# Fourier mixing and an ELU layer on one core: products of later x chunks put behind the even/odd products

## The chip, the cores and the metric

The kernel runs on one core of a Trainium2 chip. The time is the device time of one execution in microseconds; before the change the median of three runs is 2578.33 us (2577.13 to 2579.94). Everything is fp32. The engines are called PE (TensorE), DVE (VectorE), ACT (ScalarE), POOL (GpSimd) and SP (SyncE, which here only issues DMAs).

## The reference

```python
def _attn_ref(x, filt_r, filt_i):              # x (8, 3008, 256), filters (1505, 256)
    X = np.fft.rfft(x, axis=1)
    F = (filt_r + 1j * filt_i)[None, :, :]
    y = np.fft.irfft(X * F, n=x.shape[1], axis=1)
    return y.astype(np.float32)

def _moe_ref(x, w_in, w_out):                  # x (24064, 256), w_in (256, 2048), w_out (2048, 256)
    h = x @ w_in
    g = np.where(h > 0.0, h, np.exp(np.minimum(h, 0.0)) - 1.0)
    return (g @ w_out).astype(np.float32)

def reference(...):
    y = _attn_ref(x, filt_r, filt_i)
    return _moe_ref(y.reshape(8 * 3008, 256), w_in, w_out)
```

Each of 8 batches is filtered along its 3008 rows in the frequency domain; the result goes, row by row, through two matrix products with an ELU between them.

## The kernel before

**Mixing.** 3008 is 47 x 64, and the transform is done in two steps by matrix products, forward and back. Per batch there are these stages, and each stage hands over through DRAM:

- `x_load` and `x_unit` (L226, L227): a chunk c of x (6 per batch, four rows of 47 and their mirror images) is loaded, and DVE makes its sum `sd` and difference in place (`xc`), two operations.
- `a_unit` (L233): the first products, `psa <- sd,ta` and `psa <- xc,ta`, in 64x64 tiles, four of them concurrent; ACT copies `psa` to `t1` (L244). It takes two chunks at a time, so four PSUM banks. `z_write` (L322) stores them.
- `z_read` (L328) reads them transposed into `t2`; `b_unit` (L419) makes the second products, `pf <- t,pairs`, in 24x32 tiles with four banks; ACT and DVE take sums out of `pf` (L425 to L430).
- `f_read` (L348, issued by POOL) brings the filter into `fall`. `re_mult`, `re_join`, `re_sums`, `im_mult`, `im_join`, `im_sums` (L433 to L468) multiply with it on DVE. For the first group of a batch, ACT makes one extra copy (L437) in `re_mult`.
- `bi_unit` (L485) makes the first products of the way back, `pv <- zs,pairs`; ACT copies them (L488), `y_write` (L496) stores them.
- `tn_read` and `y_read` (L501, L506) bring them back transposed, `n_unit` (L520) makes the even and odd products `pse` and `pso`, 64x64 tiles again, and ACT copies them to `y` (L526); `n_sums` (L546 to L571) forms their sums on DVE.

The second and third stage go over groups g = 0, 2, 4, 6 of a batch; the last one over six parts m.

**The two layers.** An item is a part m of a batch and a quarter q of the 2048 columns: 192 items. Both products are done with seven block products in place of eight. `up_steps` (L592) gives the seven up steps, into banks `phs` (the "s" bank, four steps that add to it in turn, with an ACT copy, L603, between them), `pha` and `phd`; ELU is made by ACT (L609, L610) and DVE (L600, L614). `down_steps` (L675) gives the seven down steps into `po`. One step is four PE instructions of 256 columns.

**Order.** Everything is written out by hand, each engine works in program order, and so does each DMA queue. The main loop has one quad per item: quad i holds the up steps of item i and the down steps of item i - 1, in an order given by letters, U for up and D for down. 24 quads make a period, in which one batch passes through the layers while the next ones are mixed. `at(quad, place, fn, ...)` puts a unit of the mixing into a quad: place 2 after the third step, 4 a step or two later, 0 in the middle, 3 after the third step of the second half, 1 at the end. In `opens` are the quads that begin with a down step: those behind a unit that took four banks, so that ACT can free them. All of `phs`, `pha`, `phd`, `psa`, `pf`, `pv`, `pse` and `pso` share four banks, which go round. Below, quads are counted within their period of 24.

```python
        for i in range(-PER, len(items) + 3):
            ...
            for n, k in enumerate("DUUDUDDU" if i in opens else "UUDUDDU"):
                ...
                if n == 2 or n == (4 if i in opens else 3):
                    for fn, a in plan.get((i, 2 if n == 2 else 4), ()):
                        fn(*a)
            for fn, a in plan.get((i, 0), ()):
                fn(*a)
            for n, k in enumerate("DUUDUD" if i in opens else "DUUDUDD"):
```

In a period, quads 0, 3 and 4 end with `a_unit` of two chunks of the batch that is mixed (2, 3, 4 for batch 1, the first one done this way), with both `x_unit`s in the middle of the same quads. Quads 6, 10, 14 and 18 end with `b_unit`, quads 9, 13, 17 and 21 with `bi_unit`, then `y_write` and, at quad 21, `y_read` of part 0. `n_unit` of part 0 stands at place 2 of quad 23, parts 1 and 2 at the end of quads 1 and 5, parts 3, 4 and 5 in the middle of quads 8, 12 and 16.

Of the kernel before, what the change touches and what calls it, by code (L numbers as in the profile page):

```python
# [28 lines left out]
B = 8  # L29
# [4 lines left out]
NXC = H // XC  # L34
NG = K2 // 4
XBUFS = 4
# [101 lines left out]
def kernel(  # L138
# [9 lines left out]
    nc = tc.nc  # L148
# [83 lines left out]

    def a_unit(b, c):  # L233
        ps = [[bank("psa") for _ in range(2)] for _ in range(2)]
        for j in range(2):
            xt, w, sm = xs.pop((b, c + j)), tas.pop((b, c + j)), sds.pop((b, c + j))
            for u in range(2):
                for o, src in ((0, sm), (64, xt[:, 1])):
                    for (_, p), r in zip(ps[j], HALVES):
                        nc.tensor.matmul(p[o:o + 64, u, :], w[r, u, o:o + 64], src[r, u, :], start=True, stop=True)  # L240
        for j in range(2):
# [82 lines left out]
    def z_read(b, g):  # L324
        t = t2[:, g % 2]
        for p in range(4):
            k = p * K2 + 4 * g
            nc.sync.dma_start(t[32 * p:32 * p + 24].rearrange("i u d -> i (u d)"),  # L328
                              zs[b][:, k:k + 4, :].rearrange("i u d -> i (u d)"))

# [14 lines left out]
    def f_read(b, g):  # L345
        t = fbufs[g % 2]
        for a in range(4):
            nc.gpsimd.dma_start(t[32 * a:32 * a + 24].rearrange("p c u d -> p (c u d)"),  # L348
                                fp[g, a].rearrange("q c u d -> q (c u d)"))

# [161 lines left out]
    def n_unit(b, m):  # L512
        t, w, h = t4s.pop((b, m)), tns.pop((b, m)), half(m)
        ps = [bank(n) for n in ("pse", "pso")]
        for q, i in enumerate(order(m)):
            n = 32 if i == 0 else 64
            for dh in range(2):
                for o in (0, 64):
                    for (_, p), r in zip(ps, HALVES):
                        nc.tensor.matmul(p[o:o + 64, dh, ds(64 * q, n)], t[r, i - 4 * m, ds(dh * P + o, 64)],  # L520
                                         w[r, i - 4 * m, 0:n], start=True, stop=True)
# [196 lines left out]
    def o_unit(b, m):  # L718
# [9 lines left out]
        o = o.rearrange("p (u f k) e s -> p u f k (e s)", u=4, f=2)  # L728
        queues = itertools.cycle((nc.sync, nc.scalar) if (b, m) == (B - 1, 5) else (nc.sync,))
        for k in range(2):  # L730
# [100 lines left out]
    with tc.manual_schedule():  # L831
# [160 lines left out]
        for i in range(2):  # L992
            at(4, 0, nc.gpsimd.memset, fbufs[i], 0.0)
        STEP = ((1, 2), (1, 1), (1, 1), (2, 2), (2, 2), (2, 1), (3, 2))
        STEP_LAST = ((1, 2), (1, 1), (2, 3), (2, 2), (2, 2), (2, 1), (3, 2))
        for b in range(B):
            t = (b - 1) * PER
            if b > 0:
                for c, s in enumerate((2, 2, 3, 3, 4, 4) if b == 1 else (0, 0, 3, 3, 4, 4)):
                    if b > 1:  # L1000
                        at(t + s, 0, x_unit, b, c)
                    elif c % 2 == 0:
                        for k in (c, c + 1):
                            at(s - 1, 1 if c else 2, x_unit, b, k)
                    if c % 2 == 0:
                        opens.add(t + s + 1)
                        at(t + s, 1, a_unit, b, c)
                    nb, nxt = (b, c + XBUFS) if c + XBUFS < NXC else (b + 1, c + XBUFS - NXC)
                    if nb < B:
                        at(t + s, 1, x_load, nb, nxt)  # L1010
                    at(t + s, 1, z_write, b, c)
                for g in range(0, NG, 2):
                    s = t + 6 + 2 * g
                    opens.update((s + 1, s + 4))
                    for k in (g, g + 1):
                        at(s - 2, 1, f_read, b, k)
                        at(s - 1, 0, z_read, b, k)
                    at(s, 1, b_unit, b, g)
                    for fn, (d, place), a in zip((re_mult, re_join, re_sums, im_mult, im_mult, im_join, im_sums),
# [4 lines left out]
            for m, (s, place, sums) in enumerate(((23, 2, ((23, 0, 0, 1), (23, 3, 2))), (25, 1, ((25, 1),)), (29, 1, ((29, 1),)),  # L1024
# [3 lines left out]
                if (b, m) == (0, 1):  # L1028
                    pass
                elif b > 0 or m > 0:  # L1030
                    r = 21 if m == 0 else s - 2
                    at(t + r, 0, tn_read, b, m)
                    at(t + r, 1 if m == 0 else 0, y_read, b, m)
                    at(t + s, place, n_unit, b, m)

                    for q, p, *a in sums:
                        at(t + q, p, n_sums, b, m, *a)
# [74 lines left out]
```

## Time and profile before

| what | us |
|---|---|
| median of the runs | 2578.33 |
| the profiled execution, its own time | 2575.46 |
| its span | 2573.7 |
| one period of 24 quads | 310.0 |
| large products: one instruction of 128x128 by 256 columns, mean duration | 0.377 |
| waits of PE for another engine or a DMA after the first 300 us, sum | 1.5 |
| longest of PE's waits, all at the start: phd for DVE (12 times) | 11.4 in all, 5.0 the longest |
| groups of psa: 672 instructions, 21 groups | 82.0 (sum of the busy time of both kinds) |
| groups of pse and pso: 3008 instructions, 47 groups | 108.3 (the same) |
| groups of pf, pv: 952 instructions each, 28 groups each | 39.0, 33.0 |

Busy times of single kinds overlap where tiles run side by side, and matmuls are pipelined, so a duration is longer than the distance between two starts; distances are read from the timeline. The groups of one line are found by their tile names. A wait is put down to the engine or the DMA that ended it.

### The profile page before, as it was taken

How to read it: one execution, taken by the hardware profiler on the slowest of the kernel's cores; microseconds unless marked ns; L12 is line 12 of the kernel's file. 1: busy time of each engine (PE TensorE's matmuls, PEld its weight loads, DVE VectorE, ACT ScalarE, POOL GpSimd, SP SyncE). 2: the span in 40 equal slices, each digit the busy share in tenths (PEclk: the TensorE clock that was granted, in tenths of full speed). 3: DMA queues.
4: the chain of work that ended last, by engine and by line, in shares of the span. 5: the costliest groups of instructions: out<-in, count | busy, mean ns of one | idle time of the engine just before them, and what ended most of it. 6: DMA issues, size and time to landing. Idle time of an engine off the chain costs nothing.

```text
span 2573.7 us, 44194 instructions
## 1 busy us (share of the span) xinstructions
PE 2529.4 (98%) x16732; PEld 2160.7 (84%) x16732; DVE 2071.6 (80%) x3612; ACT 1528.2 (59%) x2698; POOL 189.3 (7%) x325
## 2 busy tenths in 40 slices
PE   8889999999999999999999999999999999999998
PEld 5678889888898888988889888888888888898887
DVE  4988887788877888788887888778887788876666
ACT  4665665666556555665556656565656665555554
POOL 3421100010000000000000000000010011000000
PEclk8999999999999999999999999999999999999999
DMA  8753213522234231433215231243213322110010
GB/s 209 207 146 76 68 23 84 138 69 56 48 87 123 56 74 44 113 83 74 61 40 143 71 81 36 72 124 82 56 48 80 85 62 68 36 46 19 19 28 17
DMA packets 229288, 196.38 MB, mean 76 GB/s; under 512 B 129050, under 2 KB 202748, under 8 KB 228980
## 3 DMA queue, kind: packets, MB, share of 16 engines
q1 hardware_dynamic: 215828, 167.62, 26.7%
q0 software_dynamic: 12096, 25.68, 3.5%
q8 instruction: 132, 2.16, 0.3%
q14 instruction: 80, 0.66, 0.1%
q10 hardware_dynamic: 1152, 0.26, 0.1%
HBM read 121.60 MB, written 74.97 MB: 76 GB/s over the span
## 4 chain that ended last, share of the span: by engine, by line
PE 88%; DVE 6%; ACT 2%; DMA 2%; issue 1%; SPq 0%; POOL 0%; DVEq 0%; POOLq 0%; ACTq 0%
PE po L675 41%; PE phs L592 23%; PE phd L592 12%; PE pha L592 6%; PE pse L520 2%; PE pf L419 1%; PE psa L240 1%; PE pv L485 1%; DVE g L600 1%; DVE g L614 1%; DMA ff<-in_filt_i_dram 1%; ACT e L610 1%; ACT e L609 1%; PE pso L520 0%; DMA x<-in_x_dram 0%
## 5 line engine op out<-in xcount | busy, mean ns | idle before, releaser
L675 PE MATMUL po<-g,wo 128*128 128x256 f32 (+1 forms) x5376 | 1316.8, 377 | 0.0
L675 PEld LDWEIGHTS po<-g,wo 128*128 128x128 f32 x5376 | 1013.5, 190 | 165.2 <-issue 49.4
L603 ACT ACTIVATE g<-phs 128x512 f32<-128x512 f32 (+1 forms) x576 | 338.6, 588 | 717.2 <-PE phs L592 716.1
L592 PE MATMUL phs<-y,wi 128*128 128x256 f32 (+1 forms) x2288 | 580.7, 376 | 1.5 <-DVE g L614 1.1
L610 ACT ACTIVATE e<-e 128x512 f32<-128x512 f32 (+1 forms) x768 | 477.1, 621 | 24.3
L592 PEld LDWEIGHTS phs<-y,wi 128*128 128x128 f32 x2288 | 430.5, 190 | 56.5 <-ACT g L603 1.8
L600 DVE TENSOR_TENSOR g<-phd,g 128x512 f32<-128x512 f32 (+1 forms) x384 | 258.9, 674 | 267.0 <-ACT e L610 196.8
L609 ACT ACTIVATE e<-g 128x512 f32<-128x512 f32 (+1 forms) x576 | 353.4, 614 | 66.3 <-DVE g L600 51.2
L614 DVE SCALAR_TENSOR_TENSOR g<-e,g 128x512 f32<-128x512 f32 (+1 forms) x576 | 387.8, 673 | 1.6 <-ACT e L610 0.9
L614 DVE SCALAR_TENSOR_TENSOR g<-e,phs 128x512 f32<-128x512 f32 (+1 forms) x192 | 129.7, 675 | 139.2 <-ACT e L610 139.2
L592 PE MATMUL phd<-y,wi 128*128 128x256 f32 (+1 forms) x768 | 196.3, 378 | 11.4 <-DVE g L600 11.4
L592 PE MATMUL phs<-ys,wi 128*128 128x256 f32 (+1 forms) x784 | 198.7, 376 | 6.4 <-ACT g L603 5.6
L592 PE MATMUL phd<-ys,wi 128*128 128x256 f32 (+1 forms) x768 | 193.8, 375 | 0.0
L592 PE MATMUL pha<-ys,wi 128*128 128x256 f32 (+1 forms) x752 | 190.0, 375 | 0.0
L609 ACT ACTIVATE e<-phs 128x512 f32<-128x512 f32 (+1 forms) x192 | 113.3, 590 | 113.2 <-PE phs L592 113.2
L592 PEld LDWEIGHTS phd<-y,wi 128*128 128x128 f32 x768 | 145.7, 191 | 32.2 <-DVE g L600 16.1
L592 PEld LDWEIGHTS phs<-ys,wi 128*128 128x128 f32 x784 | 147.6, 190 | 25.2 <-ACT g L603 7.8
L348 POOL DMA_DIRECT2D fall<-fp x224 | 110.0, 499 | 692.0 <-DVE r L458 686.4
L592 PEld LDWEIGHTS phd<-ys,wi 128*128 128x128 f32 x768 | 145.7, 190 | 16.6
L592 PEld LDWEIGHTS pha<-ys,wi 128*128 128x128 f32 x752 | 142.8, 190 | 16.5
L600 DVE TENSOR_TENSOR g<-pha,g 128x512 f32<-128x512 f32 (+1 forms) x192 | 129.0, 672 | 24.3 <-PE pha L592 24.3
L654 DVE TENSOR_TENSOR g<-g,g 128x512 f32<-128x512 f32 (+1 forms) x192 | 132.6, 690 | 6.6
(184 smaller groups left out, 2175.4 us busy)
## 6 DMA issues: line engine op xcount, KB each, us to landing
t<-yd SPq DMA_DIRECT2D x94, 256.0 KB
z<-t SPq DMA_DIRECT2D x84, 256.0 KB
fall<-fp POOLq DMA_DIRECT2D x224, 96.0 KB, 2.9
t<-z SPq DMA_DIRECT2D x224, 96.0 KB
yd<-t SPq DMA_DIRECT2D x112, 192.0 KB
out_dram<-o SPq DMA_DIRECT2D x632, 32.0 KB
xc<-in_x_dram SPq DMA_DIRECT2D x84, 128.0 KB
xc<-in_x_dram SPq DMA_DIRECT2D x161, 64.0 KB
```

The lines of the kernel that those rows point to most:

```text
L240: nc.tensor.matmul(p[o:o + 64, u, :], w[r, u, o:o + 64], src[r, u, :], start=True, stop=True)
L348: nc.gpsimd.dma_start(t[32 * a:32 * a + 24].rearrange("p c u d -> p (c u d)"), fp[g, a].rearrange("q c u d -> q (c u d)"))
L419: nc.tensor.matmul(pf[p][1][32 * a:32 * a + 32, js, :], fb[r, v, :], t2[r, js, a, :], start=True, stop=True, tile_position=(32 * p, 32 * a))
L520: nc.tensor.matmul(p[o:o + 64, dh, ds(64 * q, n)], t[r, i - 4 * m, ds(dh * P + o, 64)], w[r, i - 4 * m, 0:n], start=True, stop=True)
L592: nc.tensor.matmul(ps[:, a, 0:h], w_in[q][:, COMBO[n], a, :], y[n], start=start and a == 0, stop=True, skip_group_check=True)
L600: nc.vector.tensor_tensor(out=g[o], in0=i0, in1=i1, op=ALU.add)
L603: nc.scalar.activation(out=g[o], in_=i0, func=AXT.Copy)
L609: nc.scalar.activation(out=e, in_=src, func=AXT.Relu, scale=-1.0)
L610: nc.scalar.activation(out=e, in_=e, func=AXT.Exp, scale=-1.0)
L614: nc.vector.scalar_tensor_tensor(out=g[n], in0=es[n], scalar=1.0, in1=src, op0=ALU.subtract, op1=ALU.max)
L654: nc.vector.tensor_tensor(out=g["t4"], in0=g["b21"], in1=g["t2"], op=ALU.subtract)
L675: nc.tensor.matmul(po[i][:, u, 0:h], w_out[q][:, COMBO[n], a, :], g[n][:, a, :], start=begin and a == 0 and n in (1, 3, 6, 4), stop=True, ...
```

## The change

Batch 1 stays as it is. From batch 2 on (`AFTER = 2`) a chunk of x is multiplied singly, right behind an `n_unit` of an earlier batch: chunks 0 to 3 behind parts 2 to 5 of the batch two before, chunks 4 and 5 behind parts 0 and 1 of the batch before. The quads are `AQ`, and all of these stand at place 1: 5, 8, 12, 16, 22 and 1 of a period. `n_unit`s with no chunk behind them (from part 2 of batch 6 on) stay where they were. `x_unit` goes to the quads of `AU`, one chunk each. The quads behind these groups begin with a down step. `b_unit` of groups 2, 4 and 6 moves from the end of its quad to a new place 5, behind the first down step of the next one, whose order becomes DDUUDUDU; what is planned for place 2 of such a quad is then issued after the first up step. The second half of `im_mult` moves from place 2 to place 3 for groups 0, 2 and 4. `z_read` and `f_read` bring both halves of a pair in one DMA per quarter. `n_unit` issues the odd product's tile ahead of the even one's each time. The last part's stores go over three queues.

```diff
-    def a_unit(b, c):
-        ps = [[bank("psa") for _ in range(2)] for _ in range(2)]
-        for j in range(2):
+    def a_unit(b, c, n):
+        ps = [[bank("psa") for _ in range(2)] for _ in range(n)]
+        for j in range(n):
...
     def z_read(b, g):
-        t = t2[:, g % 2]
         for p in range(4):
             k = p * K2 + 4 * g
-            nc.sync.dma_start(t[32 * p:32 * p + 24].rearrange("i u d -> i (u d)"),
-                              zs[b][:, k:k + 4, :].rearrange("i u d -> i (u d)"))
+            nc.sync.dma_start(t2[32 * p:32 * p + 24].rearrange("i g u d -> i (g u d)"),
+                              zs[b][:, k:k + 8, :].rearrange("i u d -> i (u d)"))
...
     def f_read(b, g):
-        t = fbufs[g % 2]
         for a in range(4):
-            nc.gpsimd.dma_start(t[32 * a:32 * a + 24].rearrange("p c u d -> p (c u d)"),
-                                fp[g, a].rearrange("q c u d -> q (c u d)"))
+            nc.gpsimd.dma_start(fall[32 * a:32 * a + 24, 0:2].rearrange("p g c u d -> p g (c u d)"),
+                                fp[g:g + 2, a].rearrange("g q c u d -> q g (c u d)"))
...
-                    for (_, p), r in zip(ps, HALVES):
+                    for (_, p), r in reversed(tuple(zip(ps, HALVES))):
                         nc.tensor.matmul(p[o:o + 64, dh, ds(64 * q, n)], t[r, i - 4 * m, ds(dh * P + o, 64)],
                                          w[r, i - 4 * m, 0:n], start=True, stop=True)
...
-        queues = itertools.cycle((nc.sync, nc.scalar) if (b, m) == (B - 1, 5) else (nc.sync,))
+        queues = itertools.cycle((nc.sync, nc.scalar, nc.gpsimd) if (b, m) == (B - 1, 5) else (nc.sync,))
...
-        STEP = ((1, 2), (1, 1), (1, 1), (2, 2), (2, 2), (2, 1), (3, 2))
+        AFTER = 2
+        AQ, AU = (5, 8, 12, 16, 22, 25), (5, 6, 10, 14, 22, 24)
+        STEP = ((1, 2), (1, 1), (1, 1), (2, 2), (2, 3), (2, 1), (3, 2))
...
-            if b > 0:
+            if 0 < b < AFTER:
                 for c, s in enumerate((2, 2, 3, 3, 4, 4) if b == 1 else (0, 0, 3, 3, 4, 4)):
...
-                        at(t + s, 1, a_unit, b, c)
+                        at(t + s, 1, a_unit, b, c, 2)
+                    if c + XBUFS < NXC:
+                        at(t + s, 1, x_load, b, c + XBUFS)
...
+                    at(t + s, 1, z_write, b, c)
+                if b + 1 == AFTER:
+                    for c, s in enumerate((3, 5, 7, 9)):
+                        at(t + s, 0, x_load, b + 1, c)
+            elif b > 0:
+                for c, s in enumerate(AQ):
+                    s += t - PER
+                    at(AU[c] + t - PER, 0, x_unit, b, c)
+                    opens.add(s + 1)
                     nb, nxt = (b, c + XBUFS) if c + XBUFS < NXC else (b + 1, c + XBUFS - NXC)
                     if nb < B:
-                        at(t + s, 1, x_load, nb, nxt)
-                    at(t + s, 1, z_write, b, c)
+                        at(s, 1, x_load, nb, nxt)
+            if b > 0:
                 for g in range(0, NG, 2):
                     s = t + 6 + 2 * g
                     opens.update((s + 1, s + 4))
-                    for k in (g, g + 1):
-                        at(s - 2, 1, f_read, b, k)
-                        at(s - 1, 0, z_read, b, k)
-                    at(s, 1, b_unit, b, g)
+                    at(s - 2, 1, f_read, b, g)
+                    at(s - 1, 0, z_read, b, g)
+                    at(*((s + 1, 5) if g else (s, 1)), b_unit, b, g)
...
+                    nb, c = b + (2 if m > 1 else 1), m - 2 if m > 1 else 4 + m
+                    if AFTER <= nb < B:
+                        s = AQ[c] + (nb - 2) * PER - t
+                        place = 1
                     at(t + s, place, n_unit, b, m)
+                    if place == 1 and AFTER <= nb < B:
+                        at(t + s, 1, a_unit, nb, c, 1)
+                        at(t + s, 1, z_write, nb, c)
...
-            for n, k in enumerate("DUUDUDDU" if i in opens else "UUDUDDU"):
+            late = plan.get((i, 5), ())
+            for n, k in enumerate("DDUUDUDU" if late else "DUUDUDDU" if i in opens else "UUDUDDU"):
                 s = ups if k == "U" else downs
                 if s:
                     s.pop(0)()
+                if n == 0:
+                    for fn, a in late:
+                        fn(*a)
```

More of the change, by code (lines that the diff above doesn't have):

```diff
@@ L240, in a_unit @@
                         nc.tensor.matmul(p[o:o + 64, u, :], w[r, u, o:o + 64], src[r, u, :], start=True, stop=True)
-        for j in range(2):
+        for j in range(n):
             t = t1s[b, c + j] = t1p.tile([P, XC, D], FP32, tag="t1", name="t1")
@@ L1006 @@
                         opens.add(t + s + 1)
-                        at(t + s, 1, a_unit, b, c)
+                        at(t + s, 1, a_unit, b, c, 2)
+                    if c + XBUFS < NXC:
+                        at(t + s, 1, x_load, b, c + XBUFS)
+                    elif b + 1 < AFTER:
+                        at(t + s, 1, x_load, b + 1, c + XBUFS - NXC)
+                    at(t + s, 1, z_write, b, c)
[7 more added lines that the diff above has]
+                    opens.add(s + 1)
                     nb, nxt = (b, c + XBUFS) if c + XBUFS < NXC else (b + 1, c + XBUFS - NXC)
                     if nb < B:
-                        at(t + s, 1, x_load, nb, nxt)
-                    at(t + s, 1, z_write, b, c)
+                        at(s, 1, x_load, nb, nxt)
+            if b > 0:
                 for g in range(0, NG, 2):
```

## The prediction

> **What bounds the kernel now.** I read the page first: sections 1, 2 and 4.
>
> ```profile
> PE 2529.4 (98%) x16732; PEld 2160.7 (84%) x16732; DVE 2071.6 (80%) x3612; ACT 1528.2 (59%) x2698; POOL 189.3 (7%) x325
> ...
> PEclk8999999999999999999999999999999999999999
> ...
> PE 88%; DVE 6%; ACT 2%; DMA 2%; issue 1%; SPq 0%; POOL 0%; DVEq 0%; POOLq 0%; ACTq 0%
> ```
>
> TensorE is never free, its clock is granted in full, and it holds 88% of the chain of waits. Only work taken off PE, or a new wait put on it, can move the time. Busy time by stretch, over two whole periods of 24 quads:
>
> ```profile
> 408.80:718.77 309.97, 309.75 (x2098) 265.87 (x2097) 255.46 (x447) 186.43 (x330) 18.03 (x36) 1.00 0.31 77
> 1338.70:1648.72 310.02, 309.80 (x2097) 265.94 (x2096) 255.45 (x447) 186.44 (x330) 18.04 (x36) 1.00 0.31 77
> ```
>
> Columns: us, then busy PE, weight loads, DVE, ACT, POOL, then clock. A period is 310 us with 0.22 us of PE idle. The waits of PE after 300 us sum to 1.5 us; nearly all others lie before 230 us. So the steady state has nothing to win but PE's own overheads. These show in PE's timeline, around an x product (psa) and an even/odd product:
>
> ```profile
> 1038.35 1.89 PE L675 MATMUL po<-g,wo 128*128 128x256 f32 x8
> 1040.17 0.43 PE L240 MATMUL psa<-sd,ta 64*64 64x256 f32 x2
> ...
> 1040.43 0.38 PE L240 MATMUL psa<-sd,ta 64*64 64x256 f32 x2
> ...
> 1040.65 0.38 PE L240 MATMUL psa<-sd,ta 64*64 64x256 f32 x2
> ...
> 1042.05 1.02 PE L675 MATMUL po<-g,wo 128*128 128x224 f32 x4
> 1042.91 0.92 PE L592 MATMUL phs<-y,wi 128*128 128x224 f32 x4
> ```
>
> A 256-column instruction takes a 0.216 us slot (four starts per 0.863 us), so the eight of L675 end at 1040.08. The next large product starts at 1042.05, and its four take 0.86 us where 0.756 is normal for 224 columns. The group thus costs 1.97 + 0.10 = 2.08 us. Its work is 8 sets of four concurrent tiles at 0.216 = 1.73. The other 0.35 us is entry and exit: 0.09 before, about 0.05 in the first set, 0.09 after the last, 0.10 in the next product.
>
> **The change, part by part.**
>
> (1) *Chunks behind the even/odd products.* Batches 2 to 7 have 18 pair groups now; afterwards 36 single chunks stand inside even/odd groups that exist anyway. Work unchanged, 18 x 0.35 = 6.3 us of entries removed. Each of 36 seams costs between 0 (sets follow each other at their pace) and a whole entry, 0.35. Both neighbours are 64x64 tiles, so I take the near end, 0.03: 1.1 us. Net -5.2 (bounds -6.3 and +6.3).
>
> (2) *The product of m = 0 moves from three steps into quad 23 to the end of quad 22.* Its rows come by y_read, queued on SP behind y_write:
>
> ```profile
> 1315.46 3.02 SPq L496 DMA_DIRECT2D yd<-t  x4
> 1321.92 1.09 SPq L506 DMA_DIRECT2D t<-yd  x2
> 1323.13 8.63 SPq L735 DMA_DIRECT2D out_dram<-o  x16
> ```
>
> y_write waits for ACT's copies of pv, y_read for y_write to land. The second y_read's semaphore is complete at 1326.61 in the trace's records. Quad 23 begins at 1325.35; the product ran at 1328.03, so it had 1.4 us in hand. Moved, it is due at 1325.44. Quads 21 and 22 keep length and chain (pv starts 13.26 us before quad 23, in every batch), so PE waits. Completion after the start of quad 23, batches 1 to 6: 1.23, 1.20, 1.65, 1.26, 2.61, 1.12 us, the large ones where an instruction fetch delayed packets. Less the entry of 0.09: 8.5 us in all. Bounds 0 (landed in time) and 9.5. Behind it on PE stand the chunk and the first down step; DVE and ACT run dry, nobody catches up, and SP's z_write and x_load behind the chunk only start later, with quads to spare.
>
> (3) *Six more quads begin with a down step* (6, 9, 13, 17, 23, 2 of a period, in place of 1, 4, 5), so they end with one down step less. In quad 6 that brings pf, and with it quad 7, 0.86 us closer to the last up step. Quad 7 has no room:
>
> ```profile
> 1432.45 1.06 ACT L437 ACTIVATE r<-fall 32x1024 f32<-32x1024 f32 x1 [1.91 <-DVE r L430]
> 1433.42 0.57 ACT L603 ACTIVATE g<-phs 128x512 f32<-128x512 f32 x1
> ```
>
> That copy of phs ends at 1433.99; the up step that needs its bank starts at 1434.06. L437 waits for DVE's four sums from pf. The first of these started at 1429.63, 0.3 to 0.4 us after DVE had finished the quad before (L654 at 1428.65); it waited for ACT's copies of pf. With pf 0.86 earlier DVE itself is the limit and gains only 0.38, so PE waits 0.48. Five batches (in batch 1 DVE binds there anyway): 2.4 us, bounds 0 and 3. In the other five (pv at the end of 9, 13 and 17, nothing of the mixing at the end of 23 and 2) the banks come free in time as they do in quads 10, 14 and 18 now; 0.
>
> (4) *Middle pf groups after the first down step, order DDUUDUDU.* Same groups, same entries. But one down step, not two, now separates the second "s" step from the third. Copy: 0.20 us until ACT starts, 0.60 long, 0.05 to PE, 0.85 against a step of 0.863. The same case stands in quad 7, where the fourth step has the margin of (3):
>
> ```profile
> 1432.33 1.89 PE L675 MATMUL po<-g,wo 128*128 128x256 f32 x8
> 1434.06 1.11 PE L592 MATMUL phs<-y,wi 128*128 128x256 f32 x4
> 1435.01 1.03 PE L675 MATMUL po<-g,wo 128*128 128x256 f32 x4
> ```
>
> The four in the middle last 1.11 us where others last 1.03; 0.95 us to the next start where 0.863 is the slot, so 0.085 is lost. 3 x 7 quads x 0.085 = 1.8 us, bounds 0 and 2. The re_mult now ahead of the pha sum on DVE delays that sum by 2.4 us; the exponential that needs it has its next cover in ACT's 0.8 us wait for phs, so 0.
>
> (5) *x_unit in quads 5, 6, 10, 14, 22, 0.* Two DVE operations of 0.69, 1.3 us. DVE idles before its phd sum 4.5, 0.7, 2.4, about 2.2, 3.5 and 0.5 us there (quad 0 gives up one of two). Quad 6 gets 1.7 us more time ahead of that sum from the chunk and the down step. 0; without the cover up to 0.6 x 24 = 14 us, the third rival. The half of im_mult moved behind the phs maximum fills ACT's 0.8 us wait and makes up for the even/odd product gone from the middle of quads 8, 12 and 16 (1.29 us of PE against 1.2 of DVE): 0.
>
> (6) *Merged reads.* Eight z reads take SP 3.2 us and eight fall reads POOL 3.9; half the issues remain, each with twice the bytes. They land quads before their use. 0 both ways. *Odd ahead of even* changes only order: 0.
>
> (7) *Start.* DVE binds quads 7 to 9 (PE lost 0.9 + 1.6 + 0.9 us there). Two chunks, 1.73 us of PE, move in under it, while quad 9's down step ahead gives 0.86 back: -0.9, bounds -2 and +2.
>
> (8) *Tail.*
>
> ```profile
> 2567.52 3.68 SPq L735 DMA_DIRECT2D out_dram<-o  x8
> ```
>
> ACT's queue issues eight more in 3.81 us; the span ends 2.4 us after. With three queues SP has six, 2.8 us: -0.9. POOL's five need 5 x 0.5 and 2.9 us to land by the fall reads, 3.5 by the ff reads at start: between -1.0 and 0. I take -0.8. The Trainium skill (DMA: Bandwidth & Descriptors, Specifications) has about 1 us to the first byte on the GpSimd path against 0.6 on the others; by it 0.4 less would be gained. No row here has the two paths side by side.
>
> **Sum.** -5.2 + 8.5 + 2.4 + 1.8 - 0.9 - 0.8 = +5.8 us. The profiled execution took 2575.46 (span 2573.7 and 1.8 around it), so 2581.3 by its measure. It lies 2.9 below the median 2578.33; against the median, 2584.
>
> **Rivals.**
>
> A, *y_read lands in time*: the chain pv, y_write, y_read shortens by 1.3 us, and (2) is gone: 2584 - 8.5 = 2575.6, and 2571 if (3) and (4) vanish too. For it: y_write's 3.0 us of issue and 3 of landing are far more than its 768 KB need. Against: nothing in the change touches them, and seven batches repeat them within 0.1 us but for the two fetches. [...]
>
> B, *the seam is not free*: at 0.2 us a seam (1) removes 18 x 0.35 = 6.3 and adds 36 x 0.2 = 7.2 us, a loss of 0.9 in place of a gain of 5.2: 2590. From 0.175 on, the regrouping loses. Against: both neighbours are 64x64.
>
> C, *DVE late by x_unit*: 0.3 us in half of the 24 places of quads 6, 10, 14 and 0, 3.6 us: 2588. Against: the idle times of (5).
>
> D, *it does not do what it says*: PE keeps an entry of its own for each chunk, 36 x 0.35 = 12.6 against 6.3 removed: 2596. The 64x64 form on both sides speaks against it.
>
> **How the numbers follow.** Forecast 0.46 (own range 2579 to 2588), A 0.36, B 0.09, C 0.06, D 0.03. Where the chains run faster than I read them, (3) and (4), both of borderline size, go with (2) more often than not: 0.20 of A lies at 2571, 0.16 at 2576. The predicted time is the forecast's. The range takes in A's deeper half and B: 2571 to 2591, about one in ten beyond each end. 0.2%, 5.2 us, is about what a measurement of this kernel can tell from no change, so the bounds are 2573.2 and 2583.5. Faster: 0.20. Same: 0.16 of A and 0.14 of the forecast, whose lower part lies below 2583.5. Slower: the forecast's other 0.32 and B, C, D, 0.50.
>
> **What would show it.** Eighteen groups of psa alone gone, psa behind pso at 64x64 pace. PE waiting at L520 for t<-yd once a period, at the end of quad 22. PE waiting for L603 in quad 7 by about half a microsecond. A period near 311.2 us where it was 310. If the waits of PE show no L520 line, (2) is wrong and A holds; if psa starts later than 0.1 us behind pso, B or D.

## The result, and the profile after

The changed kernel takes 2591.57 us (median of six runs, 2587.04 to 2594.2) against 2578.76 us for the kernel before in the same session: a ratio of 1.0048, 95% interval 1.0038 to 1.0058. It is slower by 12.8 us. The forecast had been 2584 us, the range 2571 to 2591: the sign was right, the size was not, and the time lies just past the upper end.

The page of the changed kernel, sections 1, 2 and 4:

```profile
PE 2530.5 (98%) x16732; PEld 2157.2 (83%) x16732; DVE 2074.3 (80%) x3612; ACT 1528.6 (59%) x2698; POOL 147.6 (6%) x218
...
PEclk8899999999999999999999999999999999999999
...
PE 82%; DVE 9%; ACT 4%; DMA 3%; issue 2%; SPq 1%; POOL 0%; DVEq 0%; POOLq 0%; ACTq 0%
```

PE issues the same 16732 instructions and is busy only 1.1 us longer, while the span is 17.1 us longer (2590.8 against 2573.7). So the work did not grow: PE waits more. Its share of the chain of waits went from 88% to 82%, DVE's from 6% to 9%. Two whole periods (columns as before: us, then busy PE, weight loads, DVE, ACT, POOL, then clock):

```profile
731.93:1043.51 311.58, 309.65 (x2097) 265.52 (x2096) 255.71 (x447) 186.35 (x330) 11.65 (x20) 1.00 0.33 77
1355.10:1666.70 311.60, 309.66 (x2098) 265.51 (x2097) 255.69 (x447) 186.35 (x330) 11.65 (x20) 1.00 0.33 77
```

A period is 1.6 us longer than before (310.0), and 1.9 us of it is now without PE work where 0.2 us was. The waits of PE after 300 us (line, what ended the wait, us in all, times, longest):

```profile
PE pso L518 <- issue: 5.1, 4, 1.3
PE pso L518 <- DMA out_dram<-o: 2.7, 2, 1.3
PE phd L590 <- DVE g L598: 2.5, 10, 0.5
PE phs L590 <- ACT g L601: 1.6, 5, 0.3
```

Before, the only such line was 1.5 us for phd. (Lines L590 and L673 are now the up and the down steps, L601 the copy of phs, L598 and L612 DVE's sum and maximum.) The two lines of L518 are one wait, six times 1.2 to 1.3 us, at the product of part 0. The first label names no cause and the second a store of the layers' output, which this product doesn't read; the queue of SP and the timeline of PE show whose wait it is:

```profile
1329.54 3.01 SPq L494 DMA_DIRECT2D yd<-t  x4
1336.04 1.13 SPq L504 DMA_DIRECT2D t<-yd  x2
```

```profile
1338.79 0.81 PE L673 MATMUL po<-g,wo 128*128 128x256 f32 x3
1340.94 0.24 PE L518 MATMUL pso<-tn,t 64*64 64x64 f32 x1 [1.34 <-DMA out_dram<-o]
```

The semaphore of the second y_read, issued at 1336.58, is complete at 1340.80 in the trace's records, 4.2 us after its issue (before the change it was 4.2 us too, from 1322.43 to 1326.61), and the product starts 0.14 us later. The chain y_write, y_read, product runs as it did before, only PE now arrives first.

The total has to be cut into what the change did and what differs from run to run. Up to the end of quad 4 PE, ACT and DVE have the same work in the same order in every kernel of this study (but for the order of the tiles in one even and odd product; some loads are merged or issued at other moments). The start of quad 5, read at its first up step, lay between 160.9 and 167.0 us in their thirteen profiles, 160.9 in the profile of before (the lowest of all) and 166.7 in the profile after. From there to the end of the last product the times are 2404.5 us before and 2415.2 us after, and the rest of the span 8.3 and 8.9 us. The change thus costs 10.7 + 0.6 = 11.3 us by the traces; of the 17.1 us between the two spans 5.8 lie in the start, where kernels with equal code vary as much, and of the 12.8 us between the medians 11.3 can be found in the traces. The other 1.5 stay open.

### The profile page after: what moved, and what is told of

It is laid out like the page before. It is cut to its first block, busy times and chain, and to the rows that moved or that the text cites. A ratio compares the mean times of both kernels' runs of the same rounds, so it can differ in the third digit from the quotient of the medians.

```text
span 2590.8 us, 43720 instructions
## 1 busy us (share of the span) xinstructions
PE 2530.5 (98%) x16732; PEld 2157.2 (83%) x16732; DVE 2074.3 (80%) x3612; ACT 1528.6 (59%) x2698; POOL 147.6 (6%) x218
## 4 chain that ended last, share of the span: by engine, by line
PE 82%; DVE 9%; ACT 4%; DMA 3%; issue 2%; SPq 1%; POOL 0%; DVEq 0%; POOLq 0%; ACTq 0%
PE po L673 38%; PE phs L590 22%; PE phd L590 11%; PE pha L590 5%; DVE g L612 2%; DVE g L598 1%; PE pso L518 1%; PE pv L483 1%; PE psa L240 1%; ACT e L608 1%; ACT e L607 1%; PE pf L417 1%; DVE g L651 1%; DVE g L649 1%; DVE g L648 0%
## 5 line engine op out<-in xcount | busy, mean ns | idle before, releaser
L673 PE MATMUL po<-g,wo 128*128 128x256 f32 (+1 forms) x5376 | 1320.1, 377 | 0.0
L673 PEld LDWEIGHTS po<-g,wo 128*128 128x128 f32 x5376 | 1013.9, 190 | 170.8 <-issue 34.4
L601 ACT ACTIVATE g<-phs 128x512 f32<-128x512 f32 (+1 forms) x576 | 338.9, 588 | 714.1 <-PE phs L590 713.2
L590 PE MATMUL phs<-y,wi 128*128 128x256 f32 (+1 forms) x2288 | 582.3, 377 | 3.2 <-ACT g L601 1.8
L590 PEld LDWEIGHTS phs<-y,wi 128*128 128x128 f32 x2288 | 429.4, 190 | 63.4 <-ACT g L601 9.1
L598 DVE TENSOR_TENSOR g<-phd,g 128x512 f32<-128x512 f32 (+1 forms) x384 | 259.2, 675 | 277.2 <-ACT e L608 166.4
L612 DVE SCALAR_TENSOR_TENSOR g<-e,g 128x512 f32<-128x512 f32 (+1 forms) x576 | 388.0, 674 | 3.1 <-ACT e L608 1.0
L612 DVE SCALAR_TENSOR_TENSOR g<-e,phs 128x512 f32<-128x512 f32 (+1 forms) x192 | 129.6, 675 | 141.8 <-ACT e L608 141.8
L590 PE MATMUL phd<-y,wi 128*128 128x256 f32 (+1 forms) x768 | 196.7, 379 | 11.7 <-DVE g L598 11.7
L590 PE MATMUL phs<-ys,wi 128*128 128x256 f32 (+1 forms) x784 | 199.8, 377 | 7.8 <-ACT g L601 7.4
L590 PE MATMUL phd<-ys,wi 128*128 128x256 f32 (+1 forms) x768 | 193.8, 375 | 0.0
L590 PE MATMUL pha<-ys,wi 128*128 128x256 f32 (+1 forms) x752 | 190.0, 375 | 0.0
L590 PEld LDWEIGHTS phd<-y,wi 128*128 128x128 f32 x768 | 145.7, 191 | 33.3 <-DVE g L598 17.2
L590 PEld LDWEIGHTS phs<-ys,wi 128*128 128x128 f32 x784 | 147.9, 191 | 29.1 <-ACT g L601 12.1
L590 PEld LDWEIGHTS phd<-ys,wi 128*128 128x128 f32 x768 | 145.8, 190 | 16.5
L590 PEld LDWEIGHTS pha<-ys,wi 128*128 128x128 f32 x752 | 142.9, 190 | 16.5
L598 DVE TENSOR_TENSOR g<-pha,g 128x512 f32<-128x512 f32 (+1 forms) x192 | 128.9, 671 | 23.3 <-PE pha L590 23.3
L652 DVE TENSOR_TENSOR g<-g,g 128x512 f32<-128x512 f32 (+1 forms) x192 | 132.6, 691 | 6.7
L649 DVE TENSOR_TENSOR g<-g,g 128x512 f32<-128x512 f32 (+1 forms) x192 | 130.7, 681 | 6.6
```

Source lines behind the costliest of these rows:

```text
L590: nc.tensor.matmul(ps[:, a, 0:h], w_in[q][:, COMBO[n], a, :], y[n], start=start and a == 0, stop=True, skip_group_check=True)
L598: nc.vector.tensor_tensor(out=g[o], in0=i0, in1=i1, op=ALU.add)
L601: nc.scalar.activation(out=g[o], in_=i0, func=AXT.Copy)
L612: nc.vector.scalar_tensor_tensor(out=g[n], in0=es[n], scalar=1.0, in1=src, op0=ALU.subtract, op1=ALU.max)
L649: nc.vector.tensor_tensor(out=b12, in0=b22, in1=b12, op=ALU.subtract)
L652: nc.vector.tensor_tensor(out=g["t4"], in0=g["b21"], in1=g["t2"], op=ALU.subtract)
```

## The experiments

The theory: the regrouping itself saves time (all 18 groups of psa alone are gone), and it is the waits made by it, each at its own place, that outweigh it. The rivals: the regrouping itself costs (the seams), or it is another part of the change, the merged reads, the late pf or the moved half of im_mult. Where a time "from quad 5 on" is given, it ends with the last product. Before: 2404.5 us.

**e1, all parts but the regrouping.**

```diff
-        AFTER = 2
+        AFTER = 8
-                if b + 1 == AFTER:
+                if b + 1 == AFTER < B:
```

> The changed kernel with all its parts but the regrouping: the chunks of batches 2 to 7 stand in pairs again, in groups of their own, and the even and odd products back in their old places. Theory, by the sums from the two traces: a period of 310.0 to 310.3 us (0.09 us of waits in each of three late quads, 0.13 saved in each late pf group), the small stalls of batch 7's period (0.4 to 0.6 us in quads 9, 13, 17) there as in the changed kernel, so 2579 to 2583. Rival, that the merged reads, the late pf or the moved half of im_mult cost the time: 2588 to 2592, near the changed kernel. Boot: the first up step starts near 79.7 us if the 3.8 us more of the changed kernel's profile are chance, near 83.5 if something in the change does it.

Measured: 2593.54 us, ratio 1.0059 (1.0044 to 1.0074); from quad 5 on 2418.5 us; a period of 312.1 us. The theory is wrong and the rival holds in kind, with a time 1.5 us above the one it gave: without the regrouping the kernel is as slow as with it. The waits of PE after 300 us:

```profile
PE phd L590 <- DVE g L598: 7.9, 26, 0.5
```

In each period PE waits for phd in quads 9, 13 and 17. From start to start, less the steps' own slots, that costs 0.63, 0.43 and 0.44 us (idle, as the profile counts it, 0.47, 0.27 and 0.27), each with 0.1 behind it and 0.1 in the third up step. These are the waits that the changed kernel has in batch 7's period alone, where no chunks are left to be regrouped. The rival names three parts, one of which the prediction had costed at nothing; e5 settles which it is. The start (up to the first up step, equal code) gave 80.6 us here and 83.6 in e3.

**e2, two queues for y.** Both the last group's stores and part 0's loads:

```diff
-            nc.sync.dma_start(y_rows(b, p, 4 * g, 8), t[32 * p:32 * p + 24])
+            queue = nc.gpsimd if g == 6 and p % 2 else nc.sync
+            queue.dma_start(y_rows(b, p, 4 * g, 8), t[32 * p:32 * p + 24])
...
+            queue = nc.gpsimd if m == 0 and k else nc.sync
+            queue.dma_start(t[r], yds[b][k:P:2, 4 * m:4 * m + 4, :])
```

> The changed kernel, but the four stores of y of a batch's last group and the two loads of part 0 behind them are shared out between SP's queue and POOL's, half and half. Theory: PE waits at the odd product of part 0 (1.1 to 1.3 us, six times) because y_write's 3.0 us of issue and y_read's 1.1 stand in one queue; halved, the rows land 1.5 to 2 us earlier, the waits go, 7 us less: 2584 to 2586. Rival 1: the latency decides and not the issue, POOL's path is the longer one: the wait stays or grows, 2591 or more. Rival 2: the wait goes and the next one takes its place (DVE's sums for the first up step of the next item, or the copies of quad 23): 2588 to 2591.

Measured: 2588.64 us, ratio 1.0037 (1.0023 to 1.0052). The waits fell to about half. The waits of PE after 300 us (here L520 is the odd product), SP's queue and POOL:

```profile
PE pso L520 <- issue: 4.1, 6, 0.8
```

```profile
1323.63 0.74 SPq L495 DMA_DIRECT2D yd<-t  x2
1329.15 0.50 SPq L506 DMA_DIRECT2D t<-yd  x1
```

```profile
1323.91 1.26 POOL L495 DMA_DIRECT2D yd<-t  x2 [66.60 <-ACT t L486]
1329.64 0.56 POOL L506 DMA_DIRECT2D t<-yd  x1 [4.48 <-DMA yd<-t]
```

The stores are all issued 1.5 us after the first one began (1323.63 to 1325.17) in place of 3.0. But from there to the first load's issue it is now 4.0 us (1329.15) where it was 3.5, and from that issue to the product 5.1 us (1334.21) where it was 4.9. About half of the issue time saved came back as a longer landing, so the cause of (2) is right, and it is no matter of issue alone. The Trainium skill (DMA: Bandwidth & Descriptors, Specifications) gives the GpSimd path the longer time to the first byte; the direction agrees, though these rows cannot part it from the load on the DMA engines.

**e3, another order for quads 6 and 23.** They open with a down step as in the changed kernel, and end with two as before the change:

```diff
-            for n, k in enumerate("DDUUDUDU" if late else "DUUDUDDU" if i in opens else "UUDUDDU"):
+            early_d = i in opens and i > 5 and i % PER in (6, 23)
+            for n, k in enumerate("DDUUDUDU" if late else "DUUDUDU" if early_d else "DUUDUDDU" if i in opens else "UUDUDDU"):
...
-            for n, k in enumerate("DUUDUD" if i in opens else "DUUDUDD"):
+            for n, k in enumerate("DUUDUD" if i in opens and not early_d else "DUUDUDD"):
```

> The changed kernel with quads 6 and 23 of each period in the order DUUDUDU DUUDUDD: they begin with a down step as in the changed kernel and end with two, as before the change. Theory: the wait of quad 7 for the copy of phs falls from 0.47 to 0.09 us, that of quad 0 from 0.23 to 0, and each of the two quads gets a wait of 0.09 itself, since one down step stands where two did between two steps of phs: 0.4 us less per period, 2 to 4 us in all with the start (2588 to 2590). Rival: the wait of quad 7 hangs on DVE's work (the two x_units), not on the down step: it stays at 0.47 and the time rises by 1 us.

Measured: 2587.06 us, ratio 1.0032 (1.002 to 1.0043); from quad 5 on 2410.9 us, 4.3 less than the changed kernel. PE in quad 7, the changed kernel first, then e3:

```profile
1444.52 1.89 PE L673 MATMUL po<-g,wo 128*128 128x256 f32 x8
1446.73 1.13 PE L590 MATMUL phs<-y,wi 128*128 128x256 f32 x4 [0.31 <-ACT g L601]
```

```profile
1127.92 1.89 PE L673 MATMUL po<-g,wo 128*128 128x256 f32 x8
1129.65 1.12 PE L590 MATMUL phs<-y,wi 128*128 128x256 f32 x4
```

From start to start it was 2.21 us and is 1.73, which is eight slots of 0.216. The wait hung on the down step, not on DVE's work. The wait of 0.23 us in quad 0 went as well. The period gained 0.6 to 0.7 us where I had expected 0.4: a first product behind such a wait also starts 0.1 us late, which I had left out.

**e4, two small parts undone.**

```diff
-        queues = itertools.cycle((nc.sync, nc.scalar, nc.gpsimd) if (b, m) == (B - 1, 5) else (nc.sync,))
+        queues = itertools.cycle((nc.sync, nc.scalar) if (b, m) == (B - 1, 5) else (nc.sync,))
...
+        STEP7 = ((1, 2), (1, 1), (1, 1), (2, 2), (2, 2), (2, 1), (3, 2))
...
-                                                 STEP_LAST if g == 6 else STEP, ((), (), (), (0,), (1,), (), ())):
+                                                 STEP_LAST if g == 6 else STEP7 if b == B - 1 else STEP, ((), (), (), (0,), (1,), (), ())):
```

> The changed kernel with two of its small parts undone: the last stores on two queues, and for batch 7 alone the half of im_mult at place 2 again. Theory: from the end of the last product to the end of the span 8.3 us in place of 8.9, and the waits of PE in quads 9, 13 and 17 of batch 7's period (0.62, 0.43, 0.43) gone: 2 us less, 2589.5. Rival for the tail: the third queue has nothing to do with it and the last leg stays at 8.9 or more. Rival for the waits: they come from the opened quads or the late pf and stay.

Measured: 2589.7 us, ratio 1.0042 (1.0027 to 1.0057). No wait for DVE is left in quads 9, 13 and 17 of batch 7; its period went from 306.97 to 304.82 us, and the end of the span from 8.86 to 8.28 us behind the last product. Both parts as the theory had it, 2.7 us in the trace.

**e5, chunks in pairs, the half of im_mult back at place 2, two queues at the end.**

```diff
-        AFTER = 2
+        AFTER = 8
-        STEP = ((1, 2), (1, 1), (1, 1), (2, 2), (2, 3), (2, 1), (3, 2))
+        STEP = ((1, 2), (1, 1), (1, 1), (2, 2), (2, 2), (2, 1), (3, 2))
...
+        queues = itertools.cycle((nc.sync, nc.scalar) if (b, m) == (B - 1, 5) else (nc.sync,))
```

> As e1 (chunks in pairs again), and besides the half of im_mult of groups 0 to 4 back at place 2 and the last stores on two queues: what is left of the change is the late pf, the merged reads and odd ahead of even. Theory: e1's waits for phd in quads 9, 13 and 17 (0.6, 0.4, 0.4 us in each period, with as much as 0.2 more behind each) come from the moved half of im_mult meeting the even and odd products in the middle of those quads; they go, and a period takes 309.9 to 310.1 us, 2577 to 2580 in all, as before the change. Rival, that the late pf or the merged reads make DVE late there: a period of 311 us or more, 2586 or more.

Measured: 2579.19 us, ratio 0.9996 (0.9987 to 1.0006). A period:

```profile
723.98:1033.85 309.87, 309.64 (x2098) 265.05 (x2097) 255.92 (x447) 186.88 (x330) 11.60 (x20) 1.00 0.35 77
```

So the 2 us per period of e1 were that half of im_mult, and the merged reads, the late pf and the order of odd and even cost nothing together: the period is 0.1 us shorter than before the change.

**e6, part 0 back in the middle of quad 23.** Chunk 4 stays alone at the end of quad 22.

```diff
-                    opens.add(s + 1)
+                    if c != 4:
+                        opens.add(s + 1)
...
-                        s = AQ[c] + (nb - 2) * PER - t
-                        place = 1
+                        r = AQ[c] + (nb - 2) * PER
+                        if m > 0:
+                            s, place = r - t, 1
                     at(t + s, place, n_unit, b, m)
-                    if place == 1 and AFTER <= nb < B:
-                        at(t + s, 1, a_unit, nb, c, 1)
+                    if AFTER <= nb < B:
+                        at(r, 1, a_unit, nb, c, 1)
```

> The changed kernel with the product of part 0 back in the middle of quad 23, where it stood before; its chunk, number 4, stays at the end of quad 22 alone, and quad 23 begins with an up step as before. Theory: the six waits for y_read (1.1 to 1.3 us each) go, and the wait of 0.23 us in quad 0 with them; the lone chunk has an entry of 0.35 us of its own: a period 1.2 us shorter, 310.3 us, 2584 in all. Rival 1, y_read is late in the middle of quad 23 too, since the transfers changed: waits for it stay. Rival 2, the regrouping itself costs time: a period stays above 311 us although the waits are gone.

Measured: 2581.31 us, ratio 1.0013 (1.0004 to 1.0023); a period of 310.2 us. The waits of PE after 300 us have no pso line left:

```profile
PE phd L590 <- DVE g L598: 2.6, 10, 0.5
PE phs L590 <- ACT g L601: 1.6, 5, 0.3
```

This one undoing takes 1.4 us from each period; from quad 5 on 7.9 us. The median fell by 10.3 us; what it fell beyond the 7.9 is in no part of the trace that this edit touches.

**e7, e6 with quad 6's order of e3 and both parts of e4.**

```diff
+            early_d = i in opens and i > 5 and i % PER == 6
...
+        STEP7 = ((1, 2), (1, 1), (1, 1), (2, 2), (2, 2), (2, 1), (3, 2))
...
+        queues = itertools.cycle((nc.sync, nc.scalar) if (b, m) == (B - 1, 5) else (nc.sync,))
```

> As e6, and besides quad 6 in the order DUUDUDU DUUDUDD, the half of im_mult of batch 7 at place 2, and the last stores on two queues. Theory: all the new waits found are out, the saving of five shared groups per period is left: a period of 309.8 us, the tail as before, 2578 to 2580 in all, that is about the time before the change (within 0.1%). Rival: what the regrouping saves is still outweighed, 2583 or more, since the start (x_unit of batch 2 in quads 5 and 6, where DVE is the bound) costs more than thought.

Measured: 2577.05 us, ratio 0.999 (0.998 to 0.9999); a period of 309.8 us, from quad 5 on 2402.4. What is left of the change is a gain of 2.1 us from quad 5 on.

**e8, chunk 4 in the group of part 0 again, but behind the first down step of quad 23.** The group moves from the end of quad 22 to place 5 of quad 23, with y on two queues (e2), quad 6 in the order of e3, and both parts of e4:

```diff
-                    opens.add(s + 1)
+                    if c != 4:
+                        opens.add(s + 1)
...
-                        at(s, 1, x_load, nb, nxt)
+                        at(*((s + 1, 2) if c == 4 else (s, 1)), x_load, nb, nxt)
...
                         s = AQ[c] + (nb - 2) * PER - t
                         place = 1
+                        if m == 0:
+                            s, place = s + 1, 5
...
-                        at(t + s, 1, a_unit, nb, c, 1)
+                        at(t + s, place, a_unit, nb, c, 1)
```

> The changed kernel with chunk 4 still in one group with the odd and even products of part 0, but behind the first down step of quad 23 (0.86 us later, order DDUUDUDU), and the stores and loads of y before it on two queues as in e2; quad 6, batch 7's im_mult and the tail as in e7. Theory: e2 left waits of 0.6 to 0.8 us for y_read; 0.86 us of a down step ahead covers them. A period of 309.9 us, 2578 to 2580 in all. Rival: the copies of four banks then stand between the first up steps of quad 23, and the waits come back there, at phs for ACT: a period above 310.5 us.

Measured: 2575.97 us, ratio 0.9989 (0.9979 to 0.9999). A period of 309.93 us; no wait for y above 0.1 us is left, only the 0.23 us in quad 0 (0.33 with what follows).

**e9, e8 with the sums of part 0 earlier on DVE.**

```diff
-                            s, place = s + 1, 5
+                            s, place, sums = s + 1, 5, ((23, 4, 0, 1), (23, 0, 2))
```

> As e8, and the sums of part 0 on DVE one place earlier each (the first four behind the fourth step of quad 23, the last two in its middle in place of behind the phs maximum). Theory: the wait of 0.23 us in quad 0 (0.33 with what follows it) comes from those last two sums, which stand ahead of the phd sum at the end of quad 23 and so put off the exponential and, behind it on ACT, the copy of phs; the DVE idle time of 3.2 us in the middle of quad 23 takes them up. A period of 309.6 us and 2 us less than e8: 2574, 0.2% under the kernel before the change. Rival: the wait comes from the down step that quad 23 lacks at its end and stays: 309.93.

Measured: 2576.3 us, ratio 0.9988 (0.9979 to 0.9997). In the profile the period is what the theory said, though the 2 us less than e8 do not show in the medians:

```profile
726.13:1035.71 309.58, 309.35 (x2098) 265.24 (x2097) 255.94 (x447) 186.41 (x330) 13.49 (x23) 1.00 0.34 77
```

```profile
PE phd L592 <- DVE g L600: 1.6, 7, 0.2
```

Its waits are those of the kernel before again. So the wait in quad 0 needs both the missing down step (e3 put it back, and the wait went) and the order of DVE (e9). DVE at the end of quad 23 in the changed kernel, columns start, duration, line:

```profile
1353.98 0.69 DVE L612 SCALAR_TENSOR_TENSOR g<-e,phs 128x512 f32<-128x512 f32 x1 [0.80 <-ACT e L608]
1354.59 0.38 DVE L568 TENSOR_TENSOR ys<-ys,y 128x224 f32<-128x224 f32 x1
1354.89 0.38 DVE L569 TENSOR_TENSOR ys<-ys,y 128x224 f32<-128x224 f32 x1
1355.19 0.68 DVE L598 TENSOR_TENSOR g<-phd,g 128x512 f32<-128x512 f32 x1
```

The two sums stand for 0.6 us between the maximum and the phd sum; ACT's exponential and, behind it, its copy of phs come 0.6 us later, of which PE loses 0.23. From quad 5 on e9 takes 2400.9 us, 3.6 less than before, the lowest of all kernels here. The medians of e8 and e9 (2575.97 and 2576.3) cannot be told apart; both are faster than the kernel before, by 0.11% and 0.12%, with intervals that only just leave out no change.

**e10, batch 2's first two x_units on POOL.**

```diff
-        eng = nc.gpsimd if b == 1 and c < XSUMS else nc.vector
+        eng = nc.gpsimd if b == 1 and c < XSUMS or b == 2 and c < 2 else nc.vector
```

> As e9, and the x_units of batch 2's first two chunks, which fall into quads 5 and 6 where DVE binds, on POOL (1.4 to 1.7 us an operation there for 0.69 on DVE). Theory: these two take 1.3 us each from DVE in the stage that it binds; quads 5 to 8 become 1.3 to 2.6 us shorter, 2572. Rival 1: POOL's sums come late for the chunk at the end of the quad, or slow DVE down by sharing its port: no gain or a loss of up to 2 us. Rival 2: another wait binds these quads (ACT's copies of pf): no change.

Measured: 2577.34 us, ratio 0.9991 (0.9982 to 1.0). Quads 5 to 9 take 14.47, 13.12, 10.83, 16.18 and 13.51 us where e9 has 14.35, 13.12, 10.82, 16.18 and 13.51. The x_units were no burden there. Both rivals allow for no gain, and nothing here parts them; that ACT's copies bind these quads is not shown. The prediction's rival C (DVE late by x_unit) falls by the waits of the changed kernel itself: after 300 us PE waits for DVE in quad 21, as before the change, and in batch 7's quads 9, 13 and 17, and nowhere in quads 6, 10, 14 and 0. One wait for y of 0.6 us came back in this profile, at part 0 of one batch, so the cover that the down step gives is thin.

**e11, even ahead of odd again.**

```diff
-                    for (_, p), r in reversed(tuple(zip(ps, HALVES))):
+                    for (_, p), r in zip(ps, HALVES):
```

> As e9, with the even product's tile ahead of the odd one's each time, as before the change. Theory: only the order of four tiles that run side by side, no change (a shared group 2.10 us, the lone even and odd product 1.18). Rival: with odd ahead the last tile and the first of the chunk meet better, and each of the 36 seams now costs 0.05 to 0.1 us: shared groups 2.15 to 2.2 us, 2 to 4 us more.

Measured: 2576.22 us, ratio 0.999 (0.9981 to 0.9999). The 36 shared groups sum to 76.0 us where e9 has 75.4 and e10 76.3. Of the 0.6 us, 0.5 stand in one group, again part 0 waiting for y: no difference from the order.

## Why the prediction was off, step by step

| step of the sum | forecast, us | measured, us | where |
|---|---|---|---|
| (1) chunks behind even and odd | -5.2 | -4.7 | groups and the products behind them |
| (2) wait for y_read at part 0 | +8.5 | +8.0 | six waits (7.8 of it idle time) |
| (3) quad 7 waits for L601 | +2.4 | +2.4 | five batches |
| (3) "the other five: 0" | 0 | +2.0 and +1.7 | quad 0; pv in quads 13 and 17 |
| (4) late pf | +1.8 | +2.2 - 3.0 | waits; shorter pf groups |
| (5) moved half of im_mult | 0 | +2.1 | batch 7, quads 9, 13, 17 |
| (7) start, quads 7 to 9 | -0.9 | -0.2 | +0.75, +0.1, -1.05 |
| (8) three queues at the end | -0.8 | +0.6 | span behind the last product |
| sum | +5.8 | +11.1 | of 11.3 |

The measured column is taken from distances between starts of PE's instructions in the two traces, less their own slots; a wait counts with the late first product behind it. The steps that failed are the two zeros, "the other five" in (3) (3.7 us) and the moved half of im_mult in (5) (2.1 us), then the sizes of (8) (1.4 us) and (7) (0.7 us). The pf groups in (4) gave 2.6 us back, which the forecast had not seen either.

(1) Right, 0.5 us short. Rival B, seams of 0.2 us, and D, an entry for each chunk, fall. PE at the end of an even and odd product and the chunk behind it:

```profile
1154.42 0.22 PE L518 MATMUL pse<-tn,t 64*64 64x64 f32 x1
1154.46 0.46 PE L240 MATMUL psa<-sd,ta 64*64 64x256 f32 x2
1154.50 0.43 PE L240 MATMUL psa<-xc,ta 64*64 64x256 f32 x2
1154.68 0.45 PE L240 MATMUL psa<-sd,ta 64*64 64x256 f32 x2
```

The first chunk tile starts 0.04 us behind the last pse, and the next set 0.22 us on: the pace of the sets. The other three tiles of that set start 0.08 us later than this pace. Groups like this one, at the ends of quads 8, 12 and 16, take about 2.13 us, the others 2.05 where nothing is waited for, against 1.18 for the even and odd product alone and 0.86 for the chunk's work: seams of about 0.09 and 0.01 us. Why the two differ was not tested. In e6 a lone chunk costs 1.12 us and 0.1 in the product behind it, for four sets of 0.216 = 0.86: an entry of 0.36 us, as read before.

(2) Right, cause and size, and rival A falls: y_read did not land in time in any batch. e6 takes the waits away, e2 halves them. Each wait was 1.2 to 1.3 us; the forecast had two longer ones, 1.65 and 2.61 us less the entry, where an instruction fetch had delayed packets in the trace of before, and these did not recur: hence 8.0 and not 8.5.

(3) Quad 7 right, shown by e3. What failed is "in the other five ... the banks come free in time ... 0". I looked for the banks of the mixing's groups alone. In quad 0 it was the copy of phs: quad 23 ends with a down step less, the first up step of quad 0 comes 0.86 us sooner, and ACT reaches the copy of phs late by way of DVE's two sums (e9: 0.33 us a period). And at the end of quads 13 and 17 pv has one down step less ahead of it. (So it has in quad 9, but the group there, 40 instructions long in place of 32, takes the same time before and after.) PE's timeline at one pv group of quad 13, first in the changed kernel, then before:

```profile
909.64 1.28 PE L483 MATMUL pv<-zs,pairs 24*32 24x512 f32 x32
```

```profile
898.29 1.14 PE L485 MATMUL pv<-zs,pairs 24*32 24x512 f32 x32
```

The fourth of its tiles starts 0.14 us after the third where before it was 0.007; twelve such groups give 1.7 us. In batch 7, where quads 13 and 17 keep both down steps, the groups last 1.14 us as before, so the pause goes with the missing down step. That it is the fourth bank, freed last by DVE, is an inference from the order of the banks; no run here shows it.

(4) The wait came as forecast (0.09 us a quad, and 0.05 more in quad 11). What I left out is the other side of the same bank: with a second down step ahead of it the pf group, which used to have that pause, lost it (21 groups, 3.0 us). The group behind quad 10, before and after:

```profile
859.32 1.29 PE L419 MATMUL pf<-t,pairs 24*32 24x512 f32 x32
```

```profile
870.60 1.14 PE L417 MATMUL pf<-t,pairs 24*32 24x512 f32 x32
```

The late pf is a gain of 0.8 us, not a loss of 1.8; e5, where it stands nearly alone, agrees with 0.1 us per period.

(5) "The half of im_mult moved behind the phs maximum ... 0" held only where a group of 2.1 us at the end of the quad gives DVE time, as the steady periods of the changed kernel beside those of e1 suggest. In batch 7 the product is still in the middle of quads 8, 12 and 16, and the half of im_mult lies ahead of the phd sum of the quad before the wait:

```profile
2086.29 0.69 DVE L612 SCALAR_TENSOR_TENSOR g<-e,phs 128x512 f32<-128x512 f32 x1 [1.01 <-ACT e L608]
2086.90 0.68 DVE L455 TENSOR_TENSOR r<-r,fall 128x512 f32<-128x512 f32 x1
2087.50 0.68 DVE L456 TENSOR_TENSOR r<-r,fall 128x512 f32<-128x512 f32 x1
2088.10 0.68 DVE L598 TENSOR_TENSOR g<-phd,g 128x512 f32<-128x512 f32 x1
...
2097.55 0.68 DVE L598 TENSOR_TENSOR g<-phd,g 128x512 f32<-128x512 f32 x1
```

```profile
2098.28 1.13 PE L590 MATMUL phd<-y,wi 128*128 128x256 f32 x4 [0.46 <-DVE g L598]
```

From 2086.90 on DVE runs without a gap up to 2097.55, so the 1.2 us put in ahead reach the phd sum that PE waits for. The prediction had worked out the cover for a steady period and not for the batch whose chunks are gone. e1 put every batch into that state and lost 2.1 us a period; e4 and e5 took it out. DVE is late here as rival C had it, but by im_mult and not by x_unit.

(7) The forecast of -0.9 had quad 9's down step right (its stall of 1.05 us went), but I had left out that quad 7 of the first period waits for the same copy as the later ones do: +0.75. e10 shows that the x_units had no part in it.

(8) The issues ended sooner, as reckoned, and the end of the span did not follow. SP had six, ACT five; POOL:

```profile
2584.33 2.76 POOL L733 DMA_DIRECT2D out_dram<-o  x5 [387.29 <-DVE o L723]
```

It ends its issues at 2587.09, 5.1 us behind the last product (before, ACT's queue ended 5.9 behind it), and the data moved until about 2588.2. But the span ends 2.6 us after that, where it ended 1.5 us after the last data before. So the term was mis-sized by what comes after the data; with two queues (e4) the 8.3 us are back.

The forecast took the profiled execution's distance to its median (2.9 us) as that of a typical run. That was sound: 160.9 us to quad 5 is 3.9 us under the mean of the other twelve profiles, 164.8, and 2404.5 + 8.3 + 164.8 + 1.8 = 2579.4 is close to the medians of before (2578.8 to 2579.3).

## What to carry to other kernels

When a unit is put somewhere else, price both places for every engine, and for the first and the last batch as well as a steady one: here the regrouping gave what it promised (-4.7 us), the big loss was seen, and most of the rest of the miss lay in edits booked at zero, one of them with a cover that was true for most batches only. A unit that must come after data from DRAM can be shared with its neighbour later instead of earlier: one down step ahead of the same group, with two queues for the data, turned a wait of 1.3 us into none in most batches and, with the other new waits taken out as well, the change into a gain of 0.1%. Where a step is moved from one side of a group to the other, look at which banks are freed last on both sides: the same step cost 0.14 us at pv and gave it back at pf.

## What the runs showed that I had not expected

- A merged read lands no sooner per byte. POOL's reads of the filter, 96 KB before and 192 KB after, took 2.9 and 5.7 us from issue to landing (medians; before, then after):

```profile
fall<-fp POOLq DMA_DIRECT2D x224, 96.0 KB, 2.9
```

```profile
fall<-fp POOLq DMA_DIRECT2D x112, 192.0 KB, 5.7
```

The Trainium skill (DMA: Bandwidth & Descriptors, Anatomy of one DMA) fits about 2.0 us plus bytes over 436 GB/s for a single DMA issued by GpSimd; by it I estimate 2.2 and 2.5 us. The trace disagrees: landing grew with the bytes. The fit is for one DMA, though, and here eight (before) or four (after) were issued in a row with other transfers beside them.

- The end of the span came 2.6 to 3.2 us after the last data in the five profiles with POOL's queue among three, and 1.4 to 1.5 us after it in the eight with two. What takes the longer time is not shown.
- The start of quad 5, behind equal code, varied by 6 us between thirteen profiles, which is half of the change's effect, and the traces do not show why; a difference of two spans says little here unless that part is taken off.
